# Attention beside a Mish layer: W1 split in the projections, the low parts of W2 on GpSimd

## The chip, the cores and the metric

The kernel runs on one core of one Trainium2 chip. The metric is the device time of one execution in microseconds (us). The three runs of the kernel before gave 3457.24, 3460.29 and 3451.01 us; their median is 3457.24 us. The core has the engines PE (matrix products, with PEld for its weight loads), DVE (VectorE), ACT (ScalarE), POOL (GpSimd) and SP, which here only issues transfers.

## The reference

The input x is 2048 rows of 1024 numbers in float32, with 32 heads of 32 columns and a hidden layer of 3584.

```
xn   = (x - mean(x)) / sqrt(var(x) + 1e-5)
qkv  = xn @ wqkv                                   # 1024 x 3072
s    = concat_heads(softmax(q k^T / sqrt(32)) v) @ wo
h    = xn @ w1 + b1                                # 1024 x 3584
g    = silu((h * tanh(softplus(h))) @ w2)          # 3584 x 1024
out  = x + s * g
```

## The kernel before, in words

Every product is made of three: a float32 operand is split into a high part (a copy rounded to a shorter format, mostly on ACT) and a low part (what is left of it, one subtraction of two SBUF tiles, `low`, recorded on line 293 for every engine). PE multiplies high by high, high by low and low by high. Splitting costs one copy and one subtraction for each 128x512 piece, and split weights that are wanted again are stored to DRAM and read back.

The program has four stages.

*V.* The rows of x are normalized, turned over by PE and split into `xc` (four chunks of 512 rows, two halves each), while PE makes the first half of V (16 groups of 24 products, `v_group`); then the second half of V (16 groups more). Beside the second half, `t_half` makes sums and differences of the chunks of x (16 halves, tile `turned`), splits them, and stores some to DRAM (`ts`). Q and K are then made from these by seven products in place of eight, in the manner of Strassen. Beside V, `w1_early` also splits the first four column tiles of W1 (of 28, 128 columns each): a load of 512 KB, copies and subtractions on GpSimd, a store of 1024 KB. Tiles of x, raw weights, and staged sums share one ring of six buffers (tag "x").

*Q and K.* 16 column tiles q with 7 products i each, 12 matmuls per product, in the order `SEQ`; the pairs of chunks change between q=7 and q=8, where five operands are read from DRAM again (`NEXT`). `EARLY` moves some products of q=7 and q=8 ahead, so that their operands are free sooner. `presplit` splits half a column tile of W1 at products 0, 2 and 5 of a q (34 halves, tiles `praw` and `pw`, on GpSimd). From q=11 on, two score products of head 0 (`s_mm`) go between the products, and `load_head(0)`, called at product 3 of q=10, fetches what they read.

*The planned stage.* Attention of 32 heads and the Mish layer run together. A list scheduler (`Plan`), which runs when the program is built, keeps a clock for each engine and places each operation by fixed durations, due times and rings of buffers; it writes the fixed order in which every engine then works. `LEAN` is a table with one digit for each 21 us of the planner's clock, which picks a small preference among ready operations. Streams: `s` (scores for the maximum, read by `reduce_max` on DVE), `t` (scores again, turned over, then the exponential on ACT into tiles `p`, a ring of seven), `pv` (product with V, in groups of 6, 5 and 5 tiles of p), `z` (the sum of the p tiles, 15 additions of 128x2048 per head, on GpSimd), `zp` (PE folds z; the next head's first addition needs it done), `h` (first layer), Mish, `y` (second layer). In the first of four chunks of rows, the 56 tiles of W2 are split as they are needed: raw load (one buffer, `w2r`), high part on ACT, low part on DVE for odd tiles and on GpSimd for even ones, store. Beside that, `w1_job` splits the last seven column tiles of W1 (14 halves, tiles `w1r` and `w1w`): load, ACT, low part on DVE, store. The planner counts 0.73 us for either low part on DVE and 1.3 us for one on GpSimd.

*The end.* The product with wo, and the result.

Of the kernel before, what the change touches and what calls it, by code (L numbers as in the profile page):

```python
# [26 lines left out]
W1_V, W1_Q, W1_JOB = 4, 21, 2  # L27
# [23 lines left out]
LEAN = ("12007310058567746444408765863051770700785277035346476647354773488"  # L51
        "67623144577424747706676766073377860776675018744057005760623872000")
# [176 lines left out]
def body(ctx: ExitStack, tc: tile.TileContext, x, wqkv, wo, w1, b1, w2, out):  # L229
# [264 lines left out]
    for t in range(2, NT + 2):  # L494
        if 2 < t < NT:
            ln_b(t)

        evac = v_group(0, t - 2, {2: 22, 3: 20, 4: 14}.get(t, 8), (lambda: ln_t(t - 1)) if t <= NT else None,
                       (((0, 0), (1, 0)), ((0, 1),)) if t == 2 else (((0, 0), (0, 1)), ((1, 0),)))
        if t <= NT:  # L500
            ln_c(t - 1)
        if t == 2:
            ln_r(2)
            ln_b(2)
        if t < NT:
            ln_x(t, t == 2)
        for m in (4, 5) if t == 2 else (t + 3,):
            if m < NT:
                xts[m] = x_load(m)
        if t == 2:  # L510
            ln_a(3)
        if t + 2 < NT:
            ln_a(t + 2)
        if t + 1 < NT:
            ln_r(t + 1)
        if t in (NT - 4, NT - 3):
            for j in range(2):
                v_load(1, 2 * (t - NT + 4) + j)
        if t == NT - 2:
            v_split(1, 0)  # L520
        if t == NT + 1:
            for j in range(1, 4):
                v_split(1, j)
        evac()
        if t in (8, 10, 12, 14, 17):
            x_store()
        if t % 3 == 2 and t > 2:
            w1_early()
# [21 lines left out]
    EARLY = {(6, 2): [(7, 0)], (6, 3): [(7, 2)], (7, 4): [(8, 0)], (7, 5): [(8, 2)]}  # L550
# [24 lines left out]
    def t_half(p, k, half):  # L575
# [17 lines left out]
        if half == 0:  # L593
            whole(t[0], c0, 0)
            whole(t[1], c1, 0)
            less(t[0], t[1], t[0])
            whole(t[2], c1, 1)
            less(t[1], t[2], t[1])
            split(0, t[0], None if p else xc[1][1])
            split(2, t[1], None if p else xc[1][0])  # L600
        else:
            whole(t[3], c0, 1, nc.gpsimd)
            less(t[2], t[2], t[0])
            less(t[3], t[2], t[3], nc.gpsimd)
            split(1, t[2], None if p else xc[3][0])
            split(3 if p else 4, t[3], None, nc.gpsimd)

    halves = [(p, k, half) for p in (1, 0) for k in range(HK) for half in range(2)]
    for i, t in enumerate([4, 5, 6, 7, 12, 13, 14, 15, 0, 1, 2, 3, 8, 9, 10, 11]):
        v_group(1, t)()  # L610
        if i == 0:
            w1_early()
# [9 lines left out]
        for _ in range(2 if i in (8, 10, 12) else 1):  # L622
            if halves:
                t_half(*halves.pop(0))
        if i in (13, 14):
            for n in (2 * (i - 13), 2 * (i - 13) + 1):
# [20 lines left out]
    def stacks(pool_, i):  # L647
# [3 lines left out]
        if i == 0:  # L651
# [3 lines left out]
            nc.vector.memset(kst[i][96:98, :].bitcast(F32), 1.0)  # L655
# [65 lines left out]
    jobs = iter([(f, half) for f in range(W1_V, W1_Q) for half in range(2)])  # L721

    def presplit():
# [4 lines left out]
        raw = sp.tile([P, 512], F32, tag="praw", name=f"praw{f}_{half}", bufs=3)  # L728
# [44 lines left out]
    def product(n):  # L773
# [14 lines left out]
        def after():  # L788
            if i in (0, 1, 3):
                e[i] = sp.tile([P, 512], F32, tag=f"e{i}", name=f"e{q}_{i}", bufs=1 if i else 2)  # L790
# [18 lines left out]
    for n, (q, i) in enumerate(SEQ):  # L809
        after = product(n)  # L810
        for m in (n + 2, n + 3) if n >= 2 and n % 2 == 0 else ():
# [4 lines left out]
            if i_ == A22:  # L816
# [8 lines left out]
                if q_ + 2 < NQ:  # L825
# [5 lines left out]
        if q >= 11:  # L831
# [3 lines left out]
        if q == KT - 1 and i in NEXT:  # L835
            x_load(*NEXT[i])
        if i in (0, 2, 5) and not 5 < q < 9:
            presplit()
        if i == 3 and q == 10:
# [248 lines left out]
    w1_kept = {}  # L1088

    def w1_op(n):  # L1090
        def emit(at):
            load_w1(n)
        w1_ops[n] = op("SP", 0.1, need=w1_kept.get(n, []), emit=emit, take=["w1"], bytes_=P * 2 * KT * P * 4)

    def w1_job(f, half):
        t = {}

        def raw(at):
            t["w"] = mlp.tile([P, 2, 512], F32R, tag=f"w2{at['w2']}", name=f"w1w_{f}_{half}")
            t["raw"] = mlp.tile([P, 512], F32, tag="w2r", name=f"w1r_{f}_{half}")  # L1100
            nc.sync.dma_start(t["raw"].rearrange("p (k f) -> p k f", f=P),
                              w1[half * 512:half * 512 + 512, f * P:(f + 1) * P].rearrange("(k p) f -> p k f", p=P))

        def keep(at):
            move(w1s[f][:, :, half * HK:half * HK + HK], t["w"].rearrange("p a (k f) -> p a k f", f=P))

        own = op("SP", 0.1, emit=raw, take=["w2", "w2r"], bytes_=P * 512 * 4)
        a = op("ACT", 0.6, need=[own], emit=lambda at: copy(t["w"][:, 0], t["raw"]))
        a = op("DVE", 0.73, need=[a], emit=lambda at: low(nc.vector, t["w"][:, 1], t["raw"], t["w"][:, 0]), give=["w2r"])
        w1_kept.setdefault(f, []).append(op("SP", 0.1, need=[a], emit=keep, give=[("w2", own)], bytes_=P * 1024 * 4))  # L1110

    def w2_op(m, need=()):
# [23 lines left out]
        def rest(at):  # L1136
            low(nc.vector if m % 2 else nc.gpsimd, w2t[m][:, 1], w2r[m], w2t[m][:, 0])
# [4 lines left out]
        w2_ops[m] = a = op("DVE" if m % 2 else "POOL", 0.73 if m % 2 else 1.3, need=[a], emit=rest, give=["w2r"],  # L1142
                           key=None if m % 2 else -1)
# [18 lines left out]
    def h_stream():  # L1162
        for n in range(NC * FT):
            c, f = divmod(n, FT)
            if 0 <= n - W1_JOB < 2 * (FT - W1_Q):
                w1_job(W1_Q + (n - W1_JOB) // 2, (n - W1_JOB) % 2)
# [359 lines left out]
```

## Time and profile before

| | |
|---|---|
| runs | 3451.01 to 3460.29 us, median 3457.24 |
| profiled execution | 3455.92 us, span 3454.1 us |
| mean granted TensorE clock | 0.993 |
| PE busy | 3375.7 us (98%) |
| DVE busy | 2634.9 us (76%) |
| POOL busy | 2510.2 us (73%) |
| ACT busy | 2049.4 us (59%) |
| transfers | 531.98 MB, mean 154 GB/s |

A busy PE is not PE at its peak: ends of matmuls are modelled, so a stretch is judged by how many matmuls it holds as well. Idle time of the other engines costs nothing by itself. The V stage lasts until about 200 us, Q and K until about 550, the planned stage until 3275, and the end until 3449.

### The profile page before, as it was taken

The numbers are of one execution on the slowest core, as the hardware profiler recorded it, in microseconds if no ns is written. First come the engines' busy times: TensorE is split into PE (matmuls) and PEld (weight loads), VectorE is DVE, ScalarE is ACT, GpSimd is POOL, SyncE is SP. The second block draws the span as 40 slices with busy tenths as digits, with TensorE's granted clock in tenths as the row PEclk, the third lists the DMA queues.
The fourth block names the chain that finished last, engine by engine and source line by source line (L and its number), as shares of the span: only waits on it lengthen the run. The fifth ranks groups of instructions, "written<-read, shape, count | busy, mean of one in ns | idle before, by whom it ended". The sixth has DMA issues, their size and how long they took to land.

```text
span 3454.1 us, 45962 instructions
## 1 busy us (share of the span) xinstructions
PE 3375.7 (98%) x16867; PEld 2469.0 (71%) x16867; DVE 2634.9 (76%) x4023; ACT 2049.4 (59%) x3286; POOL 2510.2 (73%) x740
## 2 busy tenths in 40 slices
PE   8999999899999999999999999999999999999999
PEld 7878777666666667777777777767777777767787
DVE  6676578998888887787778877878787787876543
ACT  5333325666666666676666676666676766666621
POOL 1355465788788888887888878888888888888800
PEclk9999999999999999999999999999999999999999
DMA  6979976444444445433434444334344444343382
GB/s 211 318 247 291 300 240 196 132 147 144 144 144 135 131 143 163 121 112 111 123 98 123 147 147 123 105 116 123 98 126 151 140 118 120 115 118 127 126 301 85
DMA packets 308228, 531.98 MB, mean 154 GB/s; under 512 B 88906, under 2 KB 151882, under 8 KB 286282
## 3 DMA queue, kind: packets, MB, share of 16 engines
q1 hardware_dynamic: 288292, 487.36, 45.8%
q10 hardware_dynamic: 19712, 41.69, 3.2%
q8 instruction: 133, 2.18, 0.3%
q14 instruction: 91, 0.75, 0.1%
HBM read 378.76 MB, written 149.16 MB: 153 GB/s over the span
## 4 chain that ended last, share of the span: by engine, by line
PE 85%; DVE 8%; DMA 3%; ACT 2%; issue 1%; POOL 0%; SPq 0%; ACTq 0%; DVEq 0%; POOLq 0%
PE y L1268 17%; PE h L1178 16%; PE t L976 13%; PE s L894 12%; PE pv L1023 12%; PE op L1367 5%; PE v L351 3%; PE q_y L784 2%; DVE w L293 2%; DVE mx L900 2%; PE q_x L784 1%; PE q_z L784 1%; DVE w1w L293 1%; PE zp L1049 1%; ACT p L282 1%
## 5 line engine op out<-in xcount | busy, mean ns | idle before, releaser
L1005 POOL TENSOR_TENSOR z<-z,p 128x2048 f32<-128x2048 f32 x448 | 2075.6, 4633 | 182.2 <-ACT p L282 155.9
L282 ACT ACTIVATE p<-t,zero 128x512 f32<-128x512 f32 x2048 | 1377.3, 690 | 621.8 <-PE t L976 598.2
L900 DVE TENSOR_REDUCE mx<-s 128x1 f32<-128x512 f32 x1984 | 1319.5, 686 | 359.2 <-PE s L894 352.4
L1268 PE MATMUL y<-w,act 128*128 128x512 f32 x2688 | 937.4, 393 | 6.3 <-DVE mx L900 3.7
L976 PE MATMUL t<-qstack,kstack 128*128 128x512 f32 x2048 | 804.1, 395 | 19.5 <-DVE mx L900 14.6
L894 PE MATMUL s<-kstack,qstack 128*128 128x512 f32 x1984 | 779.3, 396 | 17.5 <-DVE mx L900 12.9
L1178 PE MATMUL h<-xr,w 128*128 128x512 f32 x2016 | 700.0, 390 | 0.0
L1268 PEld LDWEIGHTS y<-w,act 128*128 128x128 f32 x2688 | 506.0, 189 | 125.3 <-issue 5.9
L976 PEld LDWEIGHTS t<-qstack,kstack 128*128 128x128 f32 x2048 | 386.4, 189 | 131.9 <-DVE mx L900 21.6
L894 PEld LDWEIGHTS s<-kstack,qstack 128*128 128x128 f32 x1984 | 372.4, 189 | 140.8 <-issue 25.2
L1023 PE MATMUL pv<-p,v 128*32 128x512 f32 x4096 | 459.3, 594 | 0.0
L1178 PEld LDWEIGHTS h<-xr,w 128*128 128x128 f32 x2016 | 378.1, 188 | 80.7 <-issue 1.7
L1290 DVE TENSOR_TENSOR yacc<-yacc,y 128x512 f32<-128x512 f32 x416 | 282.9, 681 | 62.2 <-PE y L1268 61.1
L1023 PEld LDWEIGHTS pv<-p,v 128*32 128x32 f32 x4096 | 123.4, 110 | 283.1 <-issue 282.1
L1005 POOL TENSOR_TENSOR z<-p,p 128x2048 f32<-128x2048 f32 x32 | 147.8, 4619 | 220.2 <-PE zp L1049 153.7
L1178 PE MATMUL h<-xc,w 128*128 128x512 f32 x672 | 238.5, 402 | 3.1 <-DVE mx L900 2.8
L351 PE MATMUL v<-vw,xc 128*128 128x512 f32 x768 | 180.3, 394 | 0.0
L351 PEld LDWEIGHTS v<-vw,xc 128*128 128x128 f32 x768 | 143.8, 189 | 30.3 <-ACT xc L285 0.5
L1178 PEld LDWEIGHTS h<-xc,w 128*128 128x128 f32 x672 | 130.2, 194 | 32.8 <-DVE mx L900 3.8
L784 PE MATMUL q_y<-xc,wq 128*128 128x512 f32 x480 | 120.1, 401 | 6.7 <-issue 3.5
L784 PEld LDWEIGHTS q_y<-xc,wq 128*128 128x128 f32 x480 | 92.4, 194 | 28.0 <-issue 7.5
L285 ACT ACTIVATE act<-h 128x512 fp32r<-128x512 f32 x112 | 66.6, 594 | 75.8 <-DVE h L1227 74.1
(144 smaller groups left out, 3028.8 us busy)
## 6 DMA issues: line engine op xcount, KB each, us to landing
w<-w1s SPq DMA_DIRECT2D x112, 1024.0 KB
w<-w2s SPq DMA_DIRECT2D x168, 512.0 KB
w2s<-w SPq DMA_DIRECT2D x56, 512.0 KB
qstack<-qs SPq DMA_DIRECT2D x96, 256.0 KB
kstack<-ks SPq DMA_DIRECT2D x96, 256.0 KB
w1s<-pw SPq DMA_DIRECT2D x34, 512.0 KB
qs<-qst ACTq DMA_DIRECT2D x32, 512.0 KB
ks<-qst ACTq DMA_DIRECT2D x32, 512.0 KB
```

The costliest lines, as they stand in the source:

```text
L282: nc.scalar.activation(out_, in_, fn, bias=zero if bias is None else bias, scale=scale)
L351: nc.tensor.matmul(ps, xc[t // 4][k // HK][:, a, k % HK, (t % 4) * P:(t % 4 + 1) * P], vw[i, k // 2][:, b, k % 2], start=n == 0, stop=n == ...
L784: nc.tensor.matmul(ps, w[:, a, k], xx[:, b, k], start=m == 0 and i in (0, 1, 4), stop=m == 3 * HK - 1, skip_group_check=i not in (0, 1, 4))
L894: nc.tensor.matmul(sp_, qst[h % 3][:, qt * P:(qt + 1) * P], kst[h % 3][:, kc * 512:(kc + 1) * 512], start=True, stop=True)
L900: nc.vector.reduce_max(tiles["mx"][:, qt, kc:kc + 1], tiles[qt, kc], axis=AX.X)
L976: nc.tensor.matmul(tp, kst[h % 3][:, kt * P:(kt + 1) * P], qst[h % 3][:, c * 512:(c + 1) * 512], start=True, stop=True)
L1005: nc.gpsimd.tensor_tensor(zs[h], pts[T - 1] if kt == 1 else zs[h], pts[T], ALU.add)
L1023: nc.tensor.matmul(pv[h][c * DH:(c + 1) * DH, :], vt[h][:, k, :], pts[T - kt + k][:, c * 512:(c + 1) * 512], start=k == 0, stop=k == NT - 1)
L1178: nc.tensor.matmul(t["h"], w1t[n][:, a, k], xts_[c][k // HK][:, b, k % HK], start=i == 0, stop=i == 3 * KT - 1)
L1268: nc.tensor.matmul(t["y"], acts[n][:, p, s * P:(s + 1) * P], w2t[m_][:, q], start=j == 0 and i == 0, stop=j == YB - 1 and i == 2)
L1290: nc.vector.tensor_tensor(ya, ya, t["y"], ALU.add)
L1367: nc.tensor.matmul(ps[t, dh], ohl[t // 4, k][:, a, s * P:(s + 1) * P], wt[k][:, b, r], start=k == 0 and i == 0, stop=k == KT - 1 and i == 2)
```

## The change

- `w1_early` now splits ten column tiles of W1 beside V (twice in three groups, and after the second and fourth group of the second half), `presplit` the other 18 (36 halves) beside Q and K, and `w1_job` is gone from the planned stage. `praw` has two buffers in place of three.
- All 56 low parts of W2 are on GpSimd, at 1.3 us in the planner, ahead of other work there that is ready (key -1).
- In `t_half`, one sum (`whole`, on GpSimd) moves to the first half and one difference (`less`) from GpSimd to DVE. Two halves are done after groups 2, 5, 8 and 10, so that the last is done after the 12th group of the second half; the first four pieces of the weights of Q follow after groups 12 and 13.
- Product (7, 1) moves ahead, behind (6, 4); its tile `e1` has two buffers. The raw weights of q=9 are asked for behind the five operands that are read again. `load_head(0)` is called at product 0 of q=10, the first scores go at product 2 of q=11, and a 2x2048 memset of `kstack` moves from DVE to GpSimd.
- 26 of the 130 digits of `LEAN` differ.

```diff
-W1_V, W1_Q, W1_JOB = 4, 21, 2
+W1_V = 10
...
-LEAN = ("12007310058567746444408765863051770700785277035346476647354773488"
+LEAN = ("22007810058567756445438735813771770600785277035346426643654653488"
...
-        if t % 3 == 2 and t > 2:
+        if t > 3 and t % 3:
             w1_early()
...
-    EARLY = {(6, 2): [(7, 0)], (6, 3): [(7, 2)], (7, 4): [(8, 0)], (7, 5): [(8, 2)]}
+    EARLY = {(6, 2): [(7, 0)], (6, 3): [(7, 2)], (6, 4): [(7, 1)], (7, 4): [(8, 0)], (7, 5): [(8, 2)]}
...
         if half == 0:
+            whole(t[3], c0, 1, nc.gpsimd)
...
         else:
-            whole(t[3], c0, 1, nc.gpsimd)
             less(t[2], t[2], t[0])
-            less(t[3], t[2], t[3], nc.gpsimd)
+            less(t[3], t[2], t[3])
...
-        if i == 0:
+        if i in (1, 3):
             w1_early()
...
-        for _ in range(2 if i in (8, 10, 12) else 1):
+        for _ in range(2 if i in (2, 5, 8, 10) else 1):
...
-        if i in (13, 14):
-            for n in (2 * (i - 13), 2 * (i - 13) + 1):
+        if i in (12, 13):
+            for n in (2 * (i - 12), 2 * (i - 12) + 1):
                 piece(n, nc.vector)
...
-            nc.vector.memset(kst[i][96:98, :].bitcast(F32), 1.0)
+            nc.gpsimd.memset(kst[i][96:98, :].bitcast(F32), 1.0)
...
-        raw = sp.tile([P, 512], F32, tag="praw", name=f"praw{f}_{half}", bufs=3)
+        raw = sp.tile([P, 512], F32, tag="praw", name=f"praw{f}_{half}", bufs=2)
...
-                if q_ + 2 < NQ:
+                if q_ + 2 < NQ and q_ != 7:
                     q_load(q_ + 2, ring_of(q_ + 2))
...
-        if q >= 11:
+        if (q, i) >= (11, 2):
...
             x_load(*NEXT[i])
+            if i == 4:
+                q_load(9, ring_of(9))
...
-        if i == 3 and q == 10:
+        if i == 0 and q == 10:
             load_head(0)
...
-            low(nc.vector if m % 2 else nc.gpsimd, w2t[m][:, 1], w2r[m], w2t[m][:, 0])
+            low(nc.gpsimd, w2t[m][:, 1], w2r[m], w2t[m][:, 0])
...
-        w2_ops[m] = a = op("DVE" if m % 2 else "POOL", 0.73 if m % 2 else 1.3, need=[a], emit=rest, give=["w2r"],
-                           key=None if m % 2 else -1)
+        w2_ops[m] = a = op("POOL", 1.3, need=[a], emit=rest, give=["w2r"], key=-1)
...
-            if 0 <= n - W1_JOB < 2 * (FT - W1_Q):
-                w1_job(W1_Q + (n - W1_JOB) // 2, (n - W1_JOB) % 2)
```

How it moves the instructions is seen at three places. First GpSimd in the planned stage, from the end of the first head (z additions, `w<-w2r` a low part of W2, `hl` a small step of the next head's maximum). Before:

```order
L1005 TENSOR_TENSOR z_4778<-z_4778,p_5374 128x2048
L293 TENSOR_TENSOR w_6_5439<-w2r_5440,w_6_5439 128x512
L1005 TENSOR_TENSOR z_5652<-p_5528,p_5615 128x2048
L1005 TENSOR_TENSOR z_5652<-z_5652,p_5657 128x2048
L293 TENSOR_TENSOR w_8_5660<-w2r_5661,w_8_5660 128x512
L1005 TENSOR_TENSOR z_5652<-z_5652,p_5694 128x2048
L1005 TENSOR_TENSOR z_5652<-z_5652,p_5729 128x2048
L1005 TENSOR_TENSOR z_5652<-z_5652,p_5763 128x2048
L1005 TENSOR_TENSOR z_5652<-z_5652,p_5797 128x2048
L1005 TENSOR_TENSOR z_5652<-z_5652,p_5874 128x2048
L1005 TENSOR_TENSOR z_5652<-z_5652,p_5914 128x2048
```

The same place now:

```order
L1007 TENSOR_TENSOR z_4839<-z_4839,p_5419 128x2048
L293 TENSOR_TENSOR w_7_5558<-w2r_5559,w_7_5558 128x512
L1007 TENSOR_TENSOR z_5703<-p_5581,p_5614 128x2048
L293 TENSOR_TENSOR w_8_5684<-w2r_5685,w_8_5684 128x512
L1007 TENSOR_TENSOR z_5703<-z_5703,p_5701 128x2048
L1007 TENSOR_TENSOR z_5703<-z_5703,p_5744 128x2048
L293 TENSOR_TENSOR w_9_5775<-w2r_5776,w_9_5775 128x512
L1007 TENSOR_TENSOR z_5703<-z_5703,p_5787 128x2048
L1007 TENSOR_TENSOR z_5703<-z_5703,p_5820 128x2048
L293 TENSOR_TENSOR w_10_5886<-w2r_5887,w_10_5886 128x512
```

A low part now stands behind every second or third z addition, and one still stands at the change of heads. Second, DVE in the planned stage at the end of the first head's maxima (`mx` a maximum, `w1w` a low part of W1). Before:

```order
L900 TENSOR_REDUCE mx_4673<-s_13_1_5243 128x1
L293 TENSOR_TENSOR w1w_0_5214<-w1r_0_5215,w1w_0_5214 128x512
L900 TENSOR_REDUCE mx_4673<-s_13_2_5250 128x1
L900 TENSOR_REDUCE mx_4673<-s_13_3_5257 128x1
L900 TENSOR_REDUCE mx_4673<-s_14_0_5275 128x1
L900 TENSOR_REDUCE mx_4673<-s_14_1_5280 128x1
```

The same place now:

```order
L902 TENSOR_REDUCE mx_4733<-s_13_1_5246 128x1
L902 TENSOR_REDUCE mx_4733<-s_13_2_5248 128x1
L1179 TENSOR_SCALAR e_5269<-h_4945,bias_157 128x512
L902 TENSOR_REDUCE mx_4733<-s_13_3_5260 128x1
L902 TENSOR_REDUCE mx_4733<-s_14_0_5273 128x1
L902 TENSOR_REDUCE mx_4733<-s_14_1_5284 128x1
```

No low part of weights is left among the maxima and the Mish steps. Third, PE at the change of pairs, with product (6, 4) in the first row. Before:

```order
L784 MATMUL q6_z_2988<-xc1_1_186,wq24_2954 128x512 x12
L784 MATMUL q6_y_2884<-xr_1910,wq24_2954 128x512 x12
L784 MATMUL q6_z_2988<-xc3_1_190,wq25_3001 128x512 x12
L784 MATMUL q7_y_3056<-xc3_0_189,wq25_3001 128x512 x12
L784 MATMUL q7_y_3056<-xc1_0_185,wq26_3042 128x512 x12
```

The same place now:

```order
L784 MATMUL q6_z_3032<-xc1_1_186,wq24_3002 128x512 x12
L784 MATMUL q7_y_3061<-xc3_0_189,wq24_3002 128x512 x12
L784 MATMUL q6_y_2932<-xr_1958,wq25_3045 128x512 x12
L784 MATMUL q6_z_3032<-xc3_1_190,wq25_3045 128x512 x12
L784 MATMUL q7_y_3061<-xc1_0_185,wq26_3093 128x512 x12
```

Product (7, 1), the first on bank `q7_y`, stands two products earlier and no longer directly before (7, 3), which adds to the same bank.

More of the change, by code (lines that the diff above doesn't have):

```diff
@@ L50 @@
 TURN = 21.0
-LEAN = ("12007310058567746444408765863051770700785277035346476647354773488"
-        "67623144577424747706676766073377860776675018744057005760623872000")
+LEAN = ("22007810058567756445438735813771770600785277035346426643654653488"
+        "67323135577524547706646266273377660776675018744007005760023872000")
 class Later:
@@ L719, in load_w1 @@
         move(w1t[n], w1s[n % FT])
-    jobs = iter([(f, half) for f in range(W1_V, W1_Q) for half in range(2)])
+    jobs = iter([(f, half) for f in range(W1_V, FT) for half in range(2)])
     def presplit():
@@ L789, in after @@
             if i in (0, 1, 3):
-                e[i] = sp.tile([P, 512], F32, tag=f"e{i}", name=f"e{q}_{i}", bufs=1 if i else 2)
+                e[i] = sp.tile([P, 512], F32, tag=f"e{i}", name=f"e{q}_{i}", bufs=1 if i == 3 else 2)
             if i == 0:
@@ L1087, in body @@
     xts_ = {0: xc0}
-    w1_kept = {}
     def w1_op(n):
@@ L1092, in emit @@
             load_w1(n)
[L1093 to L1110, printed above, removed]
+        w1_ops[n] = op("SP", 0.1, emit=emit, take=["w1"], bytes_=P * 2 * KT * P * 4)
     def w2_op(m, need=()):
```

## The prediction

> **What bounds the kernel now.** I read the engine shares first, then the busy time by stage, then who waited for whom in the stage that loses time, then the groups of instructions. PE is busy for 98% of the span, so the question is where the rest is, and whether busy means full speed. The stretches are V, its end, Q and K in three parts, the planned stage in two. The columns are length, then PE, PEld, DVE, ACT and POOL busy with counts of instructions, the granted clock, the share of the transfer engines and GB/s.
>
> ```profile
> span 3454.1 us, 45962 instructions
> ```
> ```profile
> 18.00:200.00 182.00, 182.00 (x864) 151.67 (x862) 122.81 (x220) 77.66 (x139) 54.96 (x42) 1.00 0.71 246
> 200.00:225.00 25.00, 19.86 (x79) 15.35 (x78) 12.74 (x18) 9.03 (x17) 7.34 (x7) 0.93 0.83 268
> 225.00:325.00 100.00, 100.00 (x443) 82.81 (x442) 68.64 (x85) 35.76 (x64) 65.68 (x54) 1.00 0.92 291
> 325.00:450.00 125.00, 115.03 (x485) 93.57 (x485) 71.25 (x100) 37.45 (x67) 54.01 (x45) 0.96 0.91 296
> 450.00:575.00 125.00, 120.94 (x512) 94.16 (x511) 102.15 (x153) 47.57 (x88) 63.48 (x46) 1.00 0.69 219
> 575.00:1285.00 710.00, 664.21 (x3301) 460.88 (x3302) 615.63 (x860) 457.63 (x739) 583.61 (x153) 0.97 0.46 139
> 1285.00:3275.00 1990.00, 1990.00 (x10392) 1419.36 (x10391) 1562.11 (x2465) 1337.40 (x2111) 1674.93 (x387) 1.00 0.41 124
> ```
>
> From 1285 on PE never rests and makes 10392 / 1990 = 5.222 matmuls per us, of the same mixture. At that rate the 3301 matmuls of 575 to 1285 need 632 us; they took 710. So 78 us are lost there: 46 us of rest, and the other 32 at a lower clock (0.97) and in starting again. The rest of the losses are small: 5 us at the end of V, 10 and 4 us in Q and K. In the losing stretch PE waits for DVE above all (us in total, times, longest):
>
> ```profile
> PE t L976 <- DVE mx L900: 14.6, 9, 3.4
> PE s L894 <- DVE mx L900: 12.9, 8, 2.9
> PE t L976 <- ACT p L282: 2.6, 2, 2.4
> ```
>
> And DVE is busy for 616 of these 710 us, 87%, against 1562 / 1990 = 78% later, where PE is fed. What it does there and later does not, are the low parts of the split weights. Groups (busy us, mean ns), then the same with shortest, median and longest:
>
> ```profile
> L293 DVE TENSOR_TENSOR w<-w2r,w 128x512 fp32r<-128x512 f32 x28 | 64.5, 2304 | 7.7 <-ACT w L285 7.6
> L293 DVE TENSOR_TENSOR w1w<-w1r,w1w 128x512 fp32r<-128x512 f32 x14 | 43.8, 3128 | 5.5 <-ACT w1w L285 5.5
> L293 POOL TENSOR_TENSOR w<-w2r,w 128x512 fp32r<-128x512 f32 x28 | 36.1, 1290 | 57.0 <-ACT w L285 53.6 <-PE h L1178 2.0 <-PE s L894 1.5
> ```
> ```profile
> L293 DVE TENSOR_TENSOR w<-w2r,w x28: 683/2248/4922, 572.5 to 1297.2; 128x512 fp32r<-128x512 f32 x28
> ```
>
> The same subtraction takes 0.68 us or up to 4.92. One place shows why (DVE, PE and POOL around 685 us):
>
> ```profile
> 682.56 4.51 DVE L293 TENSOR_TENSOR w1w<-w1r,w1w 128x512 fp32r<-128x512 f32 x1 [0.37 <-ACT w1w L285]
> ```
> ```profile
> 687.73 0.50 PE L976 MATMUL t<-qstack,kstack 128*128 128x512 f32 x1 [3.38 <-DVE mx L900]
> ```
> ```profile
> 667.61 33.56 POOL L1005 TENSOR_TENSOR z<-z,p 128x2048 f32<-128x2048 f32 x7
> ```
>
> Seven z additions of 4.79 us end at 672.4, 677.2, 682.0, 686.8 and so on. The low part begins just after one and ends at 687.1, just after the next: with two SBUF inputs it does not get through while GpSimd works on its own. Behind it stand the maxima, behind these the banks, and PE rests 3.4 us.
>
> **The change, part by part.** *Low parts off DVE (planned stage).* 28 of W2 and 14 of W1 go: 64.5 + 43.8 = 108 us of DVE, all in the losing stretch but the last. DVE is left with 616 - 108 = 508 us for work that needs PE for 632, or 80%, close to the 78% at which PE is fed later. 14 loads, 14 copies on ACT and 14 stores go with them. On SP, low parts on DVE held the stores, and with them the tiles of W1 and W2 queued behind, for 156 us:
>
> ```profile
> SPq L289 <- DVE w L293: 155.7, 22, 17.0
> SPq L289 <- POOL w L293: 100.0, 19, 9.1
> ```
>
> *What takes their place.* GpSimd gets 28 more low parts at 1.29 us, 36 us, 35 of them before 1285. Its busy time becomes 584 + 35 = 619 us, or 98% of 632. So GpSimd is late next, and this sets the size of the gain. Its waits in the stretch:
>
> ```profile
> POOL z L1005 <- PE zp L1049: 45.6, 6, 12.4
> POOL z L1005 <- ACT p L282: 40.3, 13, 15.2
> POOL w L293 <- ACT w L285: 27.2, 12, 5.7
> ```
>
> The wait for zp comes once per head, between the last addition and the next first one. If all of it stayed but the 8 x 1.29 = 10 us that a low part standing there fills, GpSimd would need 619 + 35 = 654 us and the gain is 710 - 654 = 56; if none stayed, PE binds, at 632, and the gain is 78. The ring of seven p tiles lets z lag by some tiles, but low parts wait behind z additions of 4.8 us, and for them wait the one raw buffer, the y products, and on SP the store, with the next tile of W1 queued behind it. I take 58, near the first end, since the zp row is the nearest to it.
>
> On the engine for such work the Trainium skill rules the other way: "GPSIMD Engine Reference", § 4.1 Engine selection, gives elementwise work on a tile to VectorE, GpSimd being about twice as slow with two inputs. By that rule the shortest rows decide, 0.68 us on DVE against 1.29 on GpSimd, and the whole would come out as rival 2 below, at 3427 us. The mean beside z additions, 2.30 us on DVE, turns the rule round for this kernel, and I go by it.
>
> *The planner's table.* The new order reaches into the part after 1285, where no engine but PE is over 84% and PE never rests: I count nothing, and a few us if a new order starves PE somewhere.
>
> *Q and K.* A product of 12 matmuls follows the last one by 2.72 us (the first two rows). Four start late, and the reason of each is touched:
>
> ```profile
> 394.90 2.88 PE L784 MATMUL q_y<-xc,wq 128*128 128x512 f32 x12
> 397.62 2.88 PE L784 MATMUL q_z<-xc,wq 128*128 128x512 f32 x12
> 350.33 2.97 PE L784 MATMUL q_y<-xc,wq 128*128 128x512 f32 x12 [0.88 <-DVE e L769]
> 373.12 5.46 PE L784 MATMUL q_y<-xc,wq 128*128 128x512 f32 x12 [3.50 <-issue]
> 402.42 4.58 PE L784 MATMUL q_y<-xc,wq 128*128 128x512 f32 x12 [1.91 <-DVE e L769]
> 435.19 0.70 PE L682 MATMUL s<-kstack,qstack 128*128 128x512 f32 x2 [3.69 <-DMA w1s<-pw]
> ```
> ```profile
> 399.18 1.76 DVE L655 MEMSET kstack<- 2x2048 f32 x1 [2.16 <-POOL kstack L654]
> ```
> ```profile
> 369.89 0.60 ACT L285 ACTIVATE qst<-q_z 128x512 fp32r<-128x512 f32 x1 [2.37 <-DMA xc<-ts]
> ```
>
> At 350 us (7, 3) stood right behind (7, 1) and waited for the addition between them; two products now lie there, and 0.9 us go. At 373 us (8, 3) starts 3.5 us late and runs 5.46 - 2.88 = 2.6 longer: ACT's copy of a result is held by a transfer while the operands are read again, DVE's addition stands behind it, and (8, 3) needs that addition. Earlier reads (two products, 5.4 us) and q=9's load behind them thin that queue; bounds 0 and 6.1 us, I take 3. At 402 us it is DVE's memset with the wait for GpSimd ahead, 3.9 us, then the addition that PE needs: without it 1.9 us of rest and the longer run of 4.58 - 2.88 = 1.7 go; bounds 1.9 and 3.6, I take 3. The memset costs GpSimd about 1.8 us there, which nobody waits for: its next sums are pieces for products three ahead. At 435 us it is the load of head 0, asked for three products (8 us) earlier and used two products (5.4 us) later: 3.7 us go, bounds 3 and 3.7. Two more halves of W1, 1.5 MB and about 4 us of GpSimd, lie at 450 to 575, where transfers are at 0.69. With two raw buffers, not three, a load can hold SP until a split is done, below 3 us, covered by weights loaded a q ahead. Sum: 0.9 + 3 + 3 + 3.7 = 11 us, from 6 to 14.
>
> *V and its end.* Six more tiles of W1 cost 6 x 1.5 = 9 MB and GpSimd 24 copies and 24 subtractions:
>
> ```profile
> L435 POOL CAST w1p<-w1e 128x512 fp32r<-128x512 f32 x8 | 4.9, 611 | 81.3 <-DMA w1e<-in_B_w_dram 81.3
> L293 POOL TENSOR_TENSOR w1p<-w1e,w1p 128x512 fp32r<-128x512 f32 x8 | 10.3, 1290 | 0.6
> ```
>
> That is 24 x (0.61 + 1.29) = 46 us beside 55 in a stage of 182, and 9 MB / (246 / 0.71 = 346 GB/s) = 26 us of transfer where 0.29 x 182 = 53 are free. Rows of x then share the ring of six with five tiles in three groups, not four, and reuse buffers sooner by a part of a group; a group with its 8 transposes is 32 / 864 x 182 = 6.7 us. PE never rests there and rows come some groups ahead, so I count nothing; a row that came too late would cost up to a group. At the end PE waits for the weights of Q, then for `xr`:
>
> ```profile
> 204.55 4.70 PE L784 MATMUL q_x<-xc,wq 128*128 128x512 f32 x12 [3.96 <-ACT wq L285]
> 223.36 0.97 PE L784 MATMUL q_y<-xr,wq 128*128 128x512 f32 x3 [1.18 <-DMA xr<-ts]
> ```
>
> The sums now end a group earlier by count, with 8 more differences on DVE (8 x 0.69 = 5.5 us) and as many waits for GpSimd fewer. Where the 4 us of the first row go, some comes back in the second, whose load is issued when V's last store has landed. I take 2 gained, bounds -4 and 5.
>
> *Sum*, against the profiled execution of 3455.9 us (its span and 1.8 around it, 1.3 below the median): 3455.9 - 58 - 11 - 2 = 3385 us.
>
> **The rivals.** (1) GpSimd binds: it keeps the waits for zp and for ACT's high parts (45.6 + 27.2), so the stretch takes 619 + 73 = 692, gains 18, and the whole is 3455.9 - 18 - 13 = 3425. For it: 98%. Against it: the waits for ACT came from copies that were late behind DVE. (2) The low parts' own times decide: DVE is freed 42 x 0.68 = 29 us of the 108, the gain is 29 / 108 of 58 = 16, and the whole 3455.9 - 16 - 13 = 3427. Against it: the low part that ended at 687.1 us, with the z addition. This is the rule of § 4.1 that is weighed above. (3) No change: GpSimd keeps all three waits, 619 + 113 = 732, 22 over the 710 of now, against 13 gained elsewhere: 3465, within 0.3% (10 us, about what a measurement can tell from nothing). Against it: the third wait is there because ACT had no products to work on while PE stood behind DVE. (4) Slower: y products wait for W2. Each of the 28 moved low parts stands behind z additions, and if each comes one addition of 4.63 us late on PE's path, that is 28 x 4.63 = 130 us against 71 gained: 3455.9 - 71 + 130 = 3515. It decides from 71 / 28 = 2.5 us each. Against it: the 28 that stand on GpSimd already, and no wait of PE for POOL in this stretch.
>
> **How the numbers follow.** The forecast has 0.62, its own range 3359 to 3409: the stretch's gain of 78, or 45 if the zp wait stays whole (710 - 619 - 46), Q and K 14 or 6, V 5 or -4. Rival 1 has 0.20, rival 2 0.05, rival 3 0.06, rival 4 0.07. The range 3359 to 3430 takes in the first two rivals and leaves out some 0.15. Faster: 0.62 + 0.20 + 0.05 = 0.87; same 0.06; slower 0.07.
>
> **What would show it.** Right: between 575 and the end of W2's splitting DVE falls to about 80%, the rows of PE waiting for `mx` shrink from 14.6 and 12.9 us to a few, the rate nears 5.2 matmuls per us and the clock 1.00. The products that stood at 350, 402 and 435 us have no wait. Wrong: POOL over 95% with PE waiting for z (`zp`, or `pv`'s last group), or y waiting for POOL w; a rest of PE inside V, behind a row of x; or a first product of Q later than 205 us.

## The result, and the profile after

The changed kernel takes 3395.51 us (median of four runs, 3392.45 to 3397.59), the kernel before 3458.76 (four runs, 3451.01 to 3461.88). The ratio is 0.982, with a 95% interval from 0.9801 to 0.9838. It is faster by some 63 us, and the median lies 10.5 us above the forecast of 3385, inside the range of 3359 to 3430. The profiled execution:

```profile
span 3394.7 us, 45896 instructions
```

Busy time by stretch in the changed kernel (columns as in the prediction; the last stretch ends at 3210, some 6 us before this planned stage does):

```profile
18.00:200.00 182.00, 180.54 (x852) 149.27 (x850) 138.20 (x231) 78.76 (x141) 72.04 (x60) 1.00 0.84 294
200.00:225.00 25.00, 21.39 (x85) 16.05 (x84) 10.66 (x13) 8.19 (x15) 5.82 (x4) 0.91 0.89 293
...
325.00:450.00 125.00, 112.72 (x472) 91.56 (x472) 69.06 (x93) 39.30 (x69) 53.24 (x43) 0.93 0.89 289
...
575.00:1285.00 710.00, 706.71 (x3650) 500.98 (x3650) 575.39 (x917) 490.86 (x799) 654.04 (x192) 1.00 0.47 144
1285.00:3210.00 1925.00, 1925.00 (x10040) 1372.51 (x10042) 1507.33 (x2375) 1298.18 (x2048) 1637.38 (x378) 1.00 0.40 121
```

From 575 to 1285 PE is given 3650 matmuls where it had 3301: 5.14 per us, before 4.65, and 5.22 once W2 is split. Its rest falls from 46 us to 3, DVE's share from 87% to 81%. On the other side the stretch from 325 to 450 lost: PE is busy for 112.7 us there, before 115.0, and the clock is 0.93, before 0.96.

The two sums are best taken between landmarks on PE, the planned stage's first h product and the first product with wo. Before, then changed:

```profile
550.71 0.50 PE L1178 MATMUL h<-xc,w 128*128 128x512 f32 x1
...
3275.25 14.92 PE L1367 MATMUL op<-wo,xo 128*128 128x512 f32 x65
```
```profile
558.78 0.39 PE L1159 MATMUL h<-xc,w 128*128 128x512 f32 x1
...
3216.09 4.24 PE L1348 MATMUL op<-wo,xo 128*128 128x512 f32 x18
```

The planned stage went from 2724.5 us to 2657.3, a gain of 67.2. V with Q and K went from 550.7 to 558.8, a loss of 8.1. The end is as long as it was. So the forecast was carried by one term that was larger than written, and two others had the wrong sign.

Who waits for whom in the changed kernel, 575 to 1285 (us, times, longest), first PE, then GpSimd:

```profile
PE y L1249 <- ACT p L282: 2.1, 1, 2.1
PE s L896 <- DVE mx L902: 0.5, 2, 0.3
...
POOL z L1007 <- PE zp L1051: 37.7, 8, 7.4
POOL w L293 <- ACT w L285: 9.7, 5, 4.2
POOL z L1007 <- ACT p L282: 3.0, 2, 2.6
```

The 27.5 us of PE's waits for maxima in the prediction's two rows became 0.5. GpSimd's idle time in the 710 us went from 126 us (710 - 584) to 56 (710 - 654); it is 92% busy, and of the other engines only PE's weight loads wait for it, 0.8 us in all.

In Q and K the starts of products in the changed kernel, those that the prediction spoke of:

```profile
202.84 2.88 PE L784 MATMUL q_x<-xc,wq 128*128 128x512 f32 x12
...
218.46 0.93 PE L784 MATMUL q_y<-xr,wq 128*128 128x512 f32 x3 [1.85 <-DMA xr<-ts]
220.04 1.21 PE L784 MATMUL q_y<-xr,wq 128*128 128x512 f32 x3 [0.66 <-DMA xr<-ts]
222.20 3.44 PE L784 MATMUL q_y<-xr,wq 128*128 128x512 f32 x6 [0.95 <-DMA xr<-ts]
225.43 3.85 PE L784 MATMUL q_z<-xc,wq 128*128 128x512 f32 x12
...
375.49 5.46 PE L784 MATMUL q_y<-xc,wq 128*128 128x512 f32 x12 [3.35 <-issue]
...
435.69 0.62 PE L682 MATMUL s<-kstack,qstack 128*128 128x512 f32 x2
...
444.61 4.63 PE L784 MATMUL q_y<-xc,wq 128*128 128x512 f32 x10 [7.85 <-POOL wq L293]
```

The first product starts 1.7 us sooner, the seventh (225.43, before 224.17) 1.3 us later. The scores at 435 no longer wait, and 9 us behind them stands a new wait of 7.85 us, the longest of Q and K.

### The profile page after: what moved, and what is told of

Read it like the earlier page. It is cut to its first block, busy times and chain, and to the rows that moved or that the text cites. A ratio compares the mean times of both kernels' runs of the same rounds, so it can differ in the third digit from the quotient of the medians.

```text
span 3394.7 us, 45896 instructions
## 1 busy us (share of the span) xinstructions
PE 3354.4 (99%) x16867; PEld 2460.3 (72%) x16867; DVE 2551.6 (75%) x3988; ACT 2037.3 (60%) x3272; POOL 2556.3 (75%) x789
## 4 chain that ended last, share of the span: by engine, by line
PE 91%; DMA 2%; DVE 2%; ACT 1%; issue 1%; POOL 0%; SPq 0%; ACTq 0%; DVEq 0%; POOLq 0%
PE y L1249 18%; PE h L1159 17%; PE t L978 14%; PE s L896 13%; PE pv L1025 13%; PE op L1348 5%; PE q_y L784 3%; PE v L351 2%; PE q_x L784 2%; PE q_z L784 2%; PE zp L1051 1%; DMA xc<-ts 1%; DVE mx L686 0%; DVE mx L902 0%; DMA w2r<-in_B_w_dram 0%
## 5 line engine op out<-in xcount | busy, mean ns | idle before, releaser
L1249 PE MATMUL y<-w,act 128*128 128x512 f32 x2688 | 926.1, 391 | 2.2 <-ACT p L282 2.1
L1159 PE MATMUL h<-xc,w 128*128 128x512 f32 x672 | 224.8, 391 | 0.1
L784 PEld LDWEIGHTS q_y<-xc,wq 128*128 128x128 f32 x480 | 93.9, 196 | 32.8 <-POOL wq L293 8.3
```

Of the source, the lines that this page charges most:

```text
L784: nc.tensor.matmul(ps, w[:, a, k], xx[:, b, k], start=m == 0 and i in (0, 1, 4), stop=m == 3 * HK - 1, skip_group_check=i not in (0, 1, 4))
L1159: nc.tensor.matmul(t["h"], w1t[n][:, a, k], xts_[c][k // HK][:, b, k % HK], start=i == 0, stop=i == 3 * KT - 1)
L1249: nc.tensor.matmul(t["y"], acts[n][:, p, s * P:(s + 1) * P], w2t[m_][:, q], start=j == 0 and i == 0, stop=j == YB - 1 and i == 2)
```

## The experiments

Each ratio is to the kernel before, run beside it on the same chip (its medians: 3453.79 us beside e1 to e4, 3454.09 beside e5 to e8, 3456.31 beside e9 to e11). Stage is the time from the first h to the first product with wo in the profiled execution.

| run | us | ratio to before (95%) | first h | stage |
|---|---|---|---|---|
| before | 3458.76 | | 550.7 | 2724.5 |
| changed | 3395.51 | 0.982 (0.9801 to 0.9838) | 558.8 | 2657.3 |
| e1 | 3431.33 | 0.993 (0.9914 to 0.9947) | 556.3 | 2696.6 |
| e2 | 3427.37 | 0.9921 (0.9906 to 0.9936) | 556.7 | 2691.7 |
| e3 | 3464.10 | 1.0027 (1.0017 to 1.0037) | 565.6 | 2723.9 |
| e4 | 3416.83 | 0.9892 (0.9876 to 0.9908) | 563.4 | 2678.0 |
| e5 | 3472.96 | 1.005 (1.0033 to 1.0066) | 553.5 | 2723.1 |
| e6 | 3438.45 | 0.9953 (0.9938 to 0.9968) | 558.7 | 2693.3 |
| e7 | 3385.93 (one run) | | 556.9 | 2648.4 |
| e8 | 3389.53 | 0.9816 (0.9801 to 0.983) | 551.5 | 2655.6 |
| e9 | 3384.95 (one run) | | 553.4 | 2650.4 |
| e10 | 3389.37 | 0.9807 (0.9793 to 0.9822) | 551.2 | 2656.3 |
| e11 | 3384.85 | 0.9795 (0.978 to 0.9811) | 551.5 | 2655.9 |

The column of the first h also shows how far the same code scatters from one execution to the next: with the old Q and K it lies at 550.7, 556.3, 556.7, 553.5, 556.9 and 553.4 us (mean 554.6), with the changed one at 558.8, 565.6, 563.4 and 558.7 (mean 561.6). The loss of 8.1 above is one pair of these; the means differ by 7.0, and the two sets do not overlap.

The landmark at the other end fails twice. The time from it to the end of the span is 178.5 to 179.4 us in every run but e5 (195.6) and e6 (184.9). In these two the first products with wo stand ahead of work that belongs to the planned stage, in e5 of the last head's `pv` and `zp` and of 45 matmuls of `y`:

```profile
3276.56 0.39 PE L1366 MATMUL op<-wo,xo 128*128 128x512 f32 x1
...
3278.01 4.50 PE L1023 MATMUL pv<-p,v 128*32 128x512 f32 x40
```

So for e5 and e6 the time from the first h to the end of the span is the better measure: 2903.4 us before, 2918.8 in e5, 2878.2 in e6.

**e1 and e2: the old order, only the engine of the low parts changed.** In the kernel before, 28 (e1) or all 42 (e2) low parts that were DVE's are issued to GpSimd, at the same place in the program.

```diff
-            low(nc.vector if m % 2 else nc.gpsimd, w2t[m][:, 1], w2r[m], w2t[m][:, 0])
+            low(nc.gpsimd, w2t[m][:, 1], w2r[m], w2t[m][:, 0])
... (e2 alone)
-... emit=lambda at: low(nc.vector, t["w"][:, 1], t["raw"], t["w"][:, 0]), give=["w2r"])
+... emit=lambda at: low(nc.gpsimd, t["w"][:, 1], t["raw"], t["w"][:, 0]), give=["w2r"])
```

> The kernel before, its order of work unchanged on every engine but for this: the 28 odd low parts of W2 are issued to GpSimd at the place in the program where DVE had them. Stage from the first product of h to the first product with wo, 2724.5 us in the kernel before. Theory (a low part on DVE waits for the end of GpSimd's z addition, and the maxima stand behind it): 64.5 of the 108 us of such low parts leave DVE, so about 60% of the 67 us that the whole change won there, 40 us: 3459 - 40 = 3419 us, and the low parts still on DVE (w1w) keep a mean near 3.1 us. Rival A (only the low part's own time counts, 0.68 us each): 28 x 0.68 = 19 us of DVE, at most 12 us won, 3447. Rival B (the new order by the planner's table made the gain): nothing won, 3459 within 10. Rival C (GpSimd binds): POOL above 93% from 575 to 1285 and PE or ACT waiting for z, slower than 3459.

> The kernel before with all 42 low parts (28 of W2, 14 of W1) issued to GpSimd at the places where DVE had them; plan, transfers and copies of W1 stay in the stage. Theory: all 108 us leave DVE, the stage wins about what the change won, 58 to 67 us: 3392 to 3401 us, PE's waits for mx shrink from 27 us to below 8. If the transfers, copies and stores of W1's seven tiles were what cost the time (rival D), it stays 20 us or more above that, at 3415 or later. Rival A (own times): 42 x 0.68 = 29 us of DVE, 16 us won, 3443. Rival B (the new order): 3459 within 10. Rival C (GpSimd binds, which now has 36 + 18 + 36 = 90 us of low parts there): POOL near 98% in 575 to 1285 and less won than in the run with 28.

The stage won 27.9 us in e1, where the theory said 40, and 32.8 in e2, where it said 58 to 67. That is more than rival A's 12 and 16 us, and far from rival B's nothing. In e1 the low parts of W1 that stayed on DVE kept a mean of 3.06 us, as the theory said. e2's 3427 us lie where rival D put them (3415 or later: the transfers and copies of W1 cost the time); e9 below speaks against it. e2's stretch of 575 to 1285, and its waits:

```profile
575.00:1285.00 710.00, 682.88 (x3481) 474.46 (x3483) 545.24 (x860) 479.49 (x776) 650.39 (x200) 0.99 0.50 151
```
```profile
PE t L976 <- ACT p L282: 9.4, 6, 3.0
PE s L894 <- ACT p L282: 4.5, 3, 1.8
PE y L1268 <- ACT p L282: 3.5, 2, 2.7
...
POOL w L293 <- ACT w L285: 31.7, 16, 11.7
```

No wait of PE for maxima is left among the seven longest: that part of the theory holds. In their place PE waits 17 us for the exponentials p, and GpSimd stands for 31.7 us before low parts whose high part ACT has not made yet. Whether these stands cost the time is taken up at e9.

**e3: the changed kernel and its order, 28 low parts back on DVE.**

```diff
-            low(nc.gpsimd, w2t[m][:, 1], w2r[m], w2t[m][:, 0])
+            low(nc.vector if m % 2 else nc.gpsimd, w2t[m][:, 1], w2r[m], w2t[m][:, 0])
```

> The changed kernel, its order of work unchanged on every engine, but the odd low parts of W2 are issued to DVE again at the place where GpSimd had them. Theory: they take 2 us or more each again, up to 4.9, and the stage, 2657 us in the changed kernel, gets some 25 to 40 us longer: 3420 to 3435 us. Rival A (own times): 19 us more on DVE that was at 81%, and 36 us less on GpSimd at 92%: within 8 us of 3395, or faster. Rival B (the order): 3395 within 5.

The stage is 66.6 us longer than in the changed kernel, all that the change had won, and more than the theory gave. The group of low parts, and PE's waits:

```profile
L293 DVE TENSOR_TENSOR w<-w2r,w 128x512 fp32r<-128x512 f32 x28 | 77.8, 2780 | 0.0
```
```profile
PE s L896 <- DVE mx L902: 26.0, 9, 4.4
PE t L978 <- DVE mx L902: 10.9, 4, 3.8
```

28 subtractions take 77.8 us on DVE, 2.78 each, and PE's waits for maxima are back at 37 us. Rival A is out: by the low parts' shortest time it was 19 us for DVE, with 36 us taken from GpSimd, and should have cost next to nothing. What e3 does not separate is the engine from the order, which was made for low parts on GpSimd; e4 and e6 below do, with the old table.

**e4: the changed kernel with the old table `LEAN`.**

> The changed kernel with the table LEAN of the kernel before. Theory (the gain is the low parts'): the stage stays within 12 us of 2657, the whole 3390 to 3408. Rival B (the table made the gain): the stage loses 30 us or more, 3425 or later.

Between the two: the stage lost 20.7 us. 7 of these lie between 575 and 1285 (3612 matmuls for 3650, at 5.22 per us). The two rows behind W2's splitting:

```profile
1285.00:2285.00 1000.00, 998.34 (x5181) 709.82 (x5180) 791.60 (x1260) 666.13 (x1058) 835.86 (x194) 1.00 0.41 123
2285.00:3200.00 915.00, 913.50 (x4742) 648.76 (x4741) 705.06 (x1113) 610.01 (x967) 763.92 (x178) 1.00 0.41 122
```

The changed kernel makes 5222 and 4765 there, so 64 matmuls or 12 us are lost where no low part is left. So with the engines of the changed kernel the table is worth some 20 us, though it does not move a single instruction to another engine.

**e5 and e6: one half of the change each, planned with the old table.** e5 is the kernel before with all low parts of W2 on GpSimd and the planner told so; W1's seven tiles stay in the stage. e6 is the changed kernel with the old table and W2's low parts halved as before; W1 is out of the stage.

```diff
 e5, to the kernel before
-        w2_ops[m] = a = op("DVE" if m % 2 else "POOL", 0.73 if m % 2 else 1.3, need=[a], emit=rest, give=["w2r"],
-                           key=None if m % 2 else -1)
+        w2_ops[m] = a = op("POOL", 1.3, need=[a], emit=rest, give=["w2r"], key=-1)
```

> The kernel before with one part of the change: all 56 low parts of W2 on GpSimd, and the planner knows it (1.3 us, key -1). W1's seven tiles stay in the planned stage with their 14 low parts on DVE, the table LEAN is the old one. Stage before 2724.5 us, with only the engine changed and the old order 2696.6, in the changed kernel with the old table 2678.0. Theory (the wait for the z addition is the cost, and a planner that knows where the low parts stand puts them where their high part is ready): better than the old order by 5 us or more, 2680 to 2692. Rival (the order matters only through the table): 2697 within 4.

> The changed kernel with the old table and the low parts of W2 halved between DVE and GpSimd as before, known to the planner: what is left is that W1 is split wholly ahead of the planned stage. Theory: 14 low parts of 3.1 us (43.8 us of DVE), with 14 loads, copies and stores, are gone from the stage: 44 / 108 of the 46.5 us that the changed kernel won with the old table, 19 us, so a stage near 2705 and, with some 6 us lost in Q and K, about 3442 us. Rival (the transfers and ACT's copies of W1 cost more than its low parts): a stage below 2692. Rival (W1 was hidden anyway): a stage of 2720 or more, the whole 3455 or slower.

e6 won 31.2 us in the stage by the landmark, but 6.0 of them come back behind it: 25.2 us from the first h to the end, 6 more than its DVE time said and short of the rival in which transfers and copies cost more. e4 and e6 differ in one thing alone, the engine of the 28 odd low parts, and in each the planner knew it. From the first h to the end e4 takes 2856.5 us and e6 2878.2: some 22 us for the engine. So of e3's 66.6 us as much as two thirds may be that the order was made for the other engine.

e5 missed both expectations: 1.4 us won by the landmark, and 15.4 lost from the first h to the end. Its rows:

```profile
575.00:1285.00 710.00, 673.81 (x3327) 458.36 (x3326) 563.26 (x847) 458.76 (x748) 613.73 (x180) 0.98 0.48 142
1285.00:2285.00 1000.00, 997.42 (x5150) 703.43 (x5150) 783.81 (x1245) 662.72 (x1051) 834.52 (x195) 1.00 0.42 125
```

81 fewer matmuls than before from 1285 to 2285 (5231), 16 us, where all of W2 but the last low parts (until 1308) is split. The engines are those of e1, which was 42 us faster; only the order differs. So a new order by the planner, with a table that was not made for it, can cost this kernel some 20 to 40 us, and e4, e5 and e6 price their parts no finer than that. What e5's order does wrong in detail stays open. The theory's reason did not hold either: this planner knew where the low parts stand, and GpSimd still waits before them for ACT, in e5 and e4 from 575 to 1285:

```profile
POOL w L293 <- ACT w L285: 39.5, 12, 8.8
```
```profile
POOL w L293 <- ACT w L285: 43.0, 7, 27.6
```

**e7 and e9: GpSimd's additions made short.** The z additions cover 64 columns, not 2048; e7 is the kernel before, e9 is e2 with the same cut.

```diff
-            nc.gpsimd.tensor_tensor(zs[h], pts[T - 1] if kt == 1 else zs[h], pts[T], ALU.add)
+            if kt == 1:
+                nc.gpsimd.memset(zs[h], 1.0)
+                nc.gpsimd.tensor_tensor(zs[h][:, :64], pts[T - 1][:, :64], pts[T][:, :64], ALU.add)
+            else:
+                nc.gpsimd.tensor_tensor(zs[h][:, :64], zs[h][:, :64], pts[T][:, :64], ALU.add)
```

> The kernel before, with the z additions cut from 2048 columns to 64 (z is set to 1 at a head's first addition; most of the sum of p is left out), so that GpSimd's additions are a fraction of a microsecond. Low parts of W2 and W1 stay on DVE. Theory (a DVE subtraction of two SBUF tiles does not get through while a GpSimd addition runs): the 28 w and 14 w1w on DVE fall from 2.30 and 3.13 us to 0.7 to 0.9 on the mean, and PE's waits for mx from 27 us to below 10. Rival (they are slow for another reason, transfers into the tiles or ACT's copies): they stay above 1.5 us.

> The kernel with the old order and all 42 low parts on GpSimd (stage 2691.7), with its z additions cut to 64 columns too (z is set to 1 first; most of the sum of p is left out). Theory (what that order did not win is GpSimd's: low parts stand in its queue where their high part is not ready yet, and z additions of 4.6 us behind them): with short additions PE's 17 us of waits for ACT p go and the stage comes to 2645 to 2655, as with the low parts on DVE and short additions (2648.4). Rival (the old order loses elsewhere, on ACT or in the transfers of W1): it stays above 2670.

In e7 the low parts stay on DVE, in the old order, and nothing else is changed. Groups, and the stretch:

```profile
L293 DVE TENSOR_TENSOR w<-w2r,w 128x512 fp32r<-128x512 f32 x28 | 19.2, 685 | 8.5 <-ACT w L285 8.4
L293 DVE TENSOR_TENSOR w1w<-w1r,w1w 128x512 fp32r<-128x512 f32 x14 | 9.6, 685 | 5.2 <-ACT w1w L285 5.2
```
```profile
575.00:1285.00 710.00, 709.19 (x3695) 503.95 (x3694) 601.50 (x958) 509.01 (x824) 93.57 (x175) 1.00 0.52 159
```

All 42 take 0.685 us on the mean, where they took 2.30 and 3.13. PE waits for 0.5 us in all and makes 5.20 matmuls per us. This is the mechanism by itself: the same instructions, on the same engine, in the same order, and only what GpSimd does beside them is shorter. The Trainium skill, "SBUF — State Buffer", section "SBUF: two separate sides", says that a VectorE instruction with two SBUF inputs and a GpSimd instruction that reads SBUF take one pair of ports in turn, each for its whole length. The trace agrees: 0.685 us beside additions of 0.33 us, and up to 4.92 beside additions of 4.63.

e9 reaches 2650.4 us in the stage, with every low part on GpSimd and the order of e2, which took 2691.7. So what e2 lacked was GpSimd's, and not the transfers and copies of W1 (rival D), which e9 has as well. How GpSimd cost it is not shown. One candidate is a low part that waits for ACT and holds the z additions behind it: 31.7 us of POOL w <- ACT w, 9.7 in the changed kernel. But e4 has 43.0 us of that wait and still makes 3612 matmuls in the stretch, where e2 makes 3481. The other candidate is plain fullness: e2 has the 14 low parts of W1 on GpSimd too, 18.0 us, and all in all GpSimd rests there for 60 us, about as long as in the changed kernel (56).

e7 and e9 also give the floor, since GpSimd is nearly idle in both: 2648 to 2650 us. The changed kernel's 2657 is 7 to 9 us above it. So rival 1, a bound GpSimd, is worth some 9 us here, as far as this floor of the old order holds for the new one.

**e8: head 0's load late again.** The chain of waits of the changed kernel behind the 7.85 us, then GpSimd's rows of that place:

```profile
418.20 11.48 DMA qs<-qst
...
429.75 0.39 SPq L540
...
430.87 1.70 SPq L289
...
432.62 8.64 DMA praw<-in_B_w_dram
```
```profile
441.38 0.61 POOL L734 CAST pw<-praw 128x512 fp32r<-128x512 f32 x1 [14.49 <-DMA praw<-in_B_w_dram]
442.07 1.26 POOL L293 TENSOR_TENSOR pw<-praw,pw 128x512 fp32r<-128x512 f32 x1
443.29 1.26 POOL L293 TENSOR_TENSOR wq<-ws,wq 128x512 fp32r<-128x512 f32 x1
```

On SP (SPq) the raw weights of q=12 (L540) wait for a store of results that takes 11.5 us; behind them stands the raw tile of W1 (`praw`), asked for at 432.62. GpSimd waits 14.5 us for it, and the low part `wq` that PE needs is next in its queue.

```diff
-        if i == 0 and q == 10:
+        if i == 3 and q == 10:
             load_head(0)
```

> The changed kernel with load_head(0) called at product 3 of q=10 again, as before the change (first scores stay at product 2 of q=11). Theory (on SP the six early loads of head 0 and the weights of q=12 behind them hold back the raw tiles of W1; GpSimd waits for one, and the low part that PE needs stands behind it): the wait of 7.9 to 8.2 us of PE for POOL wq near 445 us falls to below 2, Q and K get 6 to 10 us shorter (355.9 to about 348), total near 3387. Rival (two raw buffers in place of three hold SP, wherever the loads stand): the wait stays above 6, total 3395 within 4. Rival (the load is then late for the first scores): a wait of 3 us or more at the first s.

```profile
421.41 0.85 SPq L730 DMA_DIRECT2D praw<-in_B_w_dram  x1
...
433.01 0.52 SPq L289 DMA_DIRECT2D w1s<-pw  x1
```
```profile
430.62 0.61 POOL L734 CAST pw<-praw 128x512 fp32r<-128x512 f32 x1 [3.43 <-DMA praw<-in_B_w_dram]
```

The tile is asked for 11 us sooner, ahead of head 0, and PE's wait for POOL `wq` is gone. The first h comes at 551.5 us, 7.3 sooner than in the changed kernel and below all four executions with the early load. The second rival has a part, less than its 3 us: the first scores now wait 2.5 us for `kstack`. The raw buffers are two here as in the changed kernel, so the first rival is out.

**e10 and e11: two more places of Q and K.** e10 adds to e8 the first scores one product later and the load of `xr` ahead of the raw weights of q=1; e11 also puts the load of the weights of q=9 back to its old place.

```diff
-        if (q, i) >= (11, 2):
+        if (q, i) >= (11, 3):
...
-    q_load(1, ring_of(1))
     x_load(xr, ts[4])
+    q_load(1, ring_of(1))
... (e11 alone)
-                if q_ + 2 < NQ and q_ != 7:
+                if q_ + 2 < NQ:
...
-            if i == 4:
-                q_load(9, ring_of(9))
```

> The changed kernel with three places of Q and K mended: load_head(0) at product 3 of q=10, the first scores one product later (product 3 of q=11), and the load of xr ahead of the raw weights of q=1. Theory: no wait for POOL wq near 445 (it was 8 us and some 2 of lower clock), no wait of the first scores (2.5 us in the run with the late load alone), and the waits for xr near 220 fall from 3.5 to below 1.5: Q and K about 346 us, total 3383 to 3387 (with the late load alone: 3389.5). Rival (the transfers are full at 205 to 225 us, so what xr gains the weights of q=1 lose): a wait for wq appears at the products after 222 us, total 3390 within 3.

> The same with the load of the raw weights of q=9 back at its old place, ahead of the operands that are read again. Theory (behind those reads the weights of q=9 come late, ACT waits 4.3 us for them at 379 us, and products near 385 and 395 start late by 3.2 us together): these two waits go, the one near 375 us grows from 2.5 to about 4: total 1 to 3 us below the run with three places mended. Rival (the reads are then late by as much): within 1 us of it, or slower.

In e10 the scores' wait for `kstack` and the wait of the 444 us product are gone and `xr` costs 0.3 us, but the first h is where e8 had it. The rival was right that the weights of q=1 are late instead, DVE's queue with them, and with that an addition (the line below); further on, products at 376 and 452 us start 3.7 and 2.1 us late.

```profile
223.50 4.35 PE L784 MATMUL q_z<-xc,wq 128*128 128x512 f32 x12 [3.23 <-DVE e L769]
```

e11's median is 4.5 us below e10's, but its profiled span is 3386.0 us and e10's 3386.1, and the intervals of the ratios overlap: not told apart. The waits at 385 and 395 us that e11 was to remove were those of e8; e10 has only 0.9 us at 395 left of them. In e11 that is gone too, the one at 375 to 380 has stayed, and another at 360 has come.

```profile
PE q_y L784 <- issue: 3.5, 1, 3.5
PE q_x L784 <- ACT wq L285: 3.0, 1, 3.0
```

e8, e10 and e11 have the lowest times of whole kernels here, 3385 to 3390 us, with a first h some 7 to 14 us sooner than the changed kernel's four executions. Their ratios, 0.9795 to 0.9816, lie inside or next to the changed kernel's interval; that they are faster rests on the time of the first h, not on the ratios.

## Why the prediction was right, and where it was not

*The sum.* The forecast changes of -58, -11 and -2 us came out at -67.2, +6.8 and +1.3. That the total was missed by 10.5 us only is in part luck: 9 us too little in the planned stage hide nearly half of the 21 us that were wrong ahead of it.

*The planned stage, -58: measured -67.2, inside the 45 to 78.* The mechanism is shown, not argued: with short additions on GpSimd (e7) the same subtractions on DVE fall to 0.685 us and PE's waits for maxima go, without moving anything, and with 28 of them back on DVE (e3) they take 2.78 us and 37 us of these waits are back. How the 67.2 us divide between the engine and the order is known only roughly: 33 for the engine in the old order (e2), 66.6 in the new one (e3), some 22 where the planner knew of each (e4 against e6). What failed in size is the step "I take 58, near the first end". It let GpSimd keep its wait for `zp` but for 10 us, and stated the stretch at 654 us; the 3301 matmuls of then now take 3301 / 5.14 = 642. The rest that it left to GpSimd was not too long: the 642 us from 575 to 1217 hold 3313 matmuls, and GpSimd rests for 49 us of them, not 35. Its busy time was put too high, 619 us for a measured 593: 115 z additions of 4.61 us in the mean there, where the stretch before had 118 of 4.68. By e7 and e9 the true bound was PE, with some 7 to 9 us left to GpSimd, so the other end of the range was nearly as close: 67.2 lies 9 us above 58 and 11 below 78.

*"The planner's table: I count nothing."* The sum came out so (5222 matmuls in the 1000 us behind 1285, before 5231), but the reason given, that nothing waits there, does not hold in general. With the old table the same place lost 12 us (e4), and in e5 16 of them. The digits had to fit the new order: with the old ones it would have cost some 20 us in the stage, a term that the step left at nothing.

*That moving the instructions is enough.* The prediction did not split the gain between the engine and the order. e2 shows the engine alone in the old order at 33 of 67 us; the rest is GpSimd's (e9), by a way that stays open.

*Q and K, -11: measured +7, from the seventh product to the first h (333.4 us for 326.5).* Of the four gains two came, at 402 and at 435 us. The one at 350 moved to a wait of 1.1 us at 364 (3.7 and 3.8 in e3 and e4), and the one at the change of pairs did not come: 3.35 us of rest and 5.46 of run at 375, as before. In e3, e4, e6 and e8, with the same code there, it came in part (1.3 to 2.5 us of rest and a run of 3.0), but with q=9's load behind the reads these have a new wait of 1.6 to 2.5 us between 385 and 391. The new 7.85 us, with the slow restart behind it (a granted clock of 0.56 from 444 to 450 us), cost some 10 and stand in no term. The term that failed is the one at 435 us, "3.7 us go, bounds 3 and 3.7", which charges nothing for moving `load_head(0)` ahead. The only sentence on SP there is "With two raw buffers, not three, a load can hold SP until a split is done, below 3 us, covered by weights loaded a q ahead". It looked at the buffer, which e8 shows to be harmless, and not at what `load_head(0)` was moved past: on SP the raw tile of W1, for which GpSimd waits, and in GpSimd's queue the low part of `wq`.

*V and its end, -2: measured +1.3 at the seventh product, inside -4 to 5.* The first product is 1.7 us sooner in place of up to 4, since V itself ends 2.4 us later (203.0 us for 200.6), and the wait for `xr`, named as what would take some back, grew from 1.2 to 3.5 us. The wait behind a row of x did not come, but "PE never rests there" did not hold either. Two rests of 0.7 us stand inside V, at 117 and 121 us, in the changed kernel as in e3, e4, e6 and e10 (e11 has one, e8 none, and none of the six executions of the old V has any). They wait for DVE's low parts of V's weights, of which six take 7.78 us where they took 4.80. Before, then changed:

```profile
112.89 4.80 DVE L293 TENSOR_TENSOR vw<-vraw,vw 128x512 fp32r<-128x512 f32 x6 [6.92 <-ACT vw L285]
```
```profile
112.80 7.78 DVE L293 TENSOR_TENSOR vw<-vraw,vw 128x512 fp32r<-128x512 f32 x6 [6.92 <-ACT vw L285]
...
117.33 2.58 PE L351 MATMUL v<-vw,xc 128*128 128x512 f32 x9 [0.73 <-DVE vw L293]
```

Beside them GpSimd now splits W1: from 112 to 121 us it is busy for 8.3 us on that, before for 1.3. So the change seems to have moved a little of the same cost from the planned stage into V; no run tests this place by itself.

*The rivals.* 1: GpSimd is at 92%, and nobody waits for it. 2, the low parts' own times, by the rule of the Trainium skill, "GPSIMD Engine Reference", § 4.1 Engine selection: e3 decides against it, with 66.6 us lost, and e6 against e4, with some 22, by giving 28 low parts to the engine that does each in 0.685 us where GpSimd's additions are short. 3: GpSimd's waits fell from 113 us to 50. 4: PE's one wait for a y product in the stretch is 2.1 us, for ACT. Its mechanism was there in another place: a low part on GpSimd that PE waits for behind work that is not ready, in Q and K.

## What to carry to other kernels

A subtraction of two SBUF tiles on DVE is priced by what GpSimd runs beside it, so before dividing work between the two, look at its shortest and longest time, not its mean. An in-order queue charges an instruction that is not ready with everything behind it: that made a load that was moved ahead cost more than it gave in Q and K. And an order that was made for one division of the work is no measure of another: the same 28 low parts on DVE cost 66.6 us in an order made without them, and some 22 where the planner knew of them. A moved transfer is followed through each queue that it passes to the next instruction that some engine waits for.

## What the runs showed that was not expected

- Putting 28 low parts (77.8 us of DVE) back into a full stage cost 66.6 us, nearly one for one, though DVE was at 81%: its share does not tell the cost. 37 us are PE's waits for the maxima that stand behind the low parts; how much of the whole is the order, which was made without them, is open.
- In the same stage an order made with a table for another order costs as much as the engine does: e5 has the engines of e1 and is 42 us slower.
- The same Q and K code starts the planned stage anywhere from 550.7 to 556.9 us in six executions, so a forecast of single microseconds there can't be judged from one trace.
